# Reordering the opening and the block loop of a fused linear-attention and mixture-of-experts kernel, with the first expert matrix fetched in two halves

## The chip, the cores and the metric

The kernel runs on one core of a Trainium2 chip. The metric is device time of one execution in microseconds (us). A quoted median is over the executions of one kernel on one chip; a ratio is the mean time of one kernel's fast runs over the mean of the other's fast runs of the same rounds, so it is not quite the ratio of the two medians. Ratios carry a 95% interval in square brackets. Some executions of a kernel fall in a slower state, at a lower clock; the record marks an execution as slow when it is over 1.5% above the fastest of its kernel, and only fast ones are compared. Engines are PE (matmuls), PEld (PE's weight loads), DVE, ACT, POOL and SP; SP and POOL also issue DMA transfers here.

## The reference, cut

```python
# attention: r, k, v are (B=4, H=8, S=768, D=48), w and u are (H, D)
for t in range(S):
    cur = einsum('bhd,bhe->bhde', u * k[:, :, t], v[:, :, t])
    y[:, :, t] = einsum('bhd,bhde->bhe', r[:, :, t], state + cur)
    state = w[..., None] * state + einsum('bhd,bhe->bhde', k[:, :, t], v[:, :, t])
x = y.transpose(0, 2, 1, 3).reshape(4, 768, 384)
# one expert out of 8 for each batch entry (a whole sentence)
logits = x.mean(axis=1) @ w_gate
e = argmax(logits, axis=1)
gate_w = softmax(logits)[e]
out[b] = gate_w[b] * (relu(x[b] @ w1[e[b]]) @ w2[e[b]])     # w1 (8,384,1024), w2 (8,1024,384)
```

Which expert's weights batch b needs is known only when all of x[b] has been computed. So each batch has a moment, the *gate*, from which its weights can first be fetched.

## The kernel before

The sequence is cut into 12 blocks of 256 rows, three for each batch. A block goes through scaling of k and r (POOL), transposes (PE) copied out by ACT, scores (PE) masked by DVE, outputs and state (PE), and transposing back. After the third block of a batch come the gate, three small DVE instructions and the weight transfers, which POOL issues. One batch of expert work is 28 *jobs*: 16 of the first layer (`mm1`, which need w1) and 12 of the second (`mm2`). They stand in a list, and the block loop takes some at each `slot()`.

```python
    def gate(b):
        ...                                        # 3 matmuls into lgp
        lg = gpool.tile([128, E], FP32, tag="lg", name=f"lg{b}")
        nc.vector.tensor_copy(lg, lgp[:, 0:E])
        ...
        nc.vector.max(out=top8, in_=lg)
        nc.vector.max_index(out=idx8, in_max=top8, in_values=lg)

    def weights(b):
        ev = nc.gpsimd.value_load(idx8[0:1, 0:1], min_val=0, max_val=E - 1)
        w1 = wpool.tile([128, NCT, F], BF16, tag="w1", name=f"w1_{b}")
        nc.gpsimd.dma_start(out=..., in_=moe_w1[ds(ev, 1)]...)
        w2 = ...
        nc.gpsimd.dma_start(out=..., in_=moe_w2[ds(ev, 1)]...)
        ...
        jobs.append(lambda ft=ft, sb=sb: mm1(b, w1, ht, ft, sb))     # x16
        jobs.append(lambda ...: mm2(b, w2, ht, si, half, cell, obs)) # x12

    RATE = 8.5 / 7
    acc = [0.0, False]

    def slot():
        if acc[1]:
            acc[0] += RATE
            c = int(acc[0])
            acc[0] -= c
            moe(c)                 # the next c jobs of the list
        else:
            fill(2, 256)           # matmuls on zeros

    for g in range(NB, N):         # blocks 3 to 11; blocks 0 to 2 are written out above
        ...                        # scaling for a later block; conditions for the last blocks are left out
        transposes(g + 1, 0)
        slot()
        scores_v(g, 1, True)
        slot()
        transposes(g + 1, 1)
        ...
        scores_v(g, 0, gi == 0); add_bonus(g); evac_y(g, 0)
        slot()
        inter(g, 1); evac_y(g, 1); scores(g + 1, 0)
        slot()
        backs(g)
        slot()
        acc[1] = True              # jobs begin in block 3, after its fifth slot
        if last:
            gate(b)
            weights(b)
        scores(g + 1, 1)
        slot()
        bonus(g + 1)
        slot()
    moe(len(jobs))
```

## Time and profile before

| what | value |
|---|---|
| median of 4 executions, beside the changed kernel's | 154.63 us (154.41 to 156.17) |
| span of the profiled execution | 152.6 us |
| PE busy | 139.5 us, 91% |
| ACT, DVE, POOL busy | 83.6, 74.4, 68.5 us |
| first expert job on PE | 45.04 us |

The head of the page's second part, span and two rows of 40 equal slices, shows where PE is not full. The first row is PE's busy share in tenths, the second the granted PE clock in tenths.

```profile
span 152.6 us, 4539 instructions
...
PE   6999877956989999999999999999999999999991
...
PEclk9999999995599999999999999999999999999999
```

PE is full from the thirteenth slice on, and the clock drops to half for about two slices in the opening.

### The profile page before, as it was taken

The numbers are of one execution on the slowest core, as the hardware profiler recorded it, in microseconds if no ns is written. First come the engines' busy times: TensorE is split into PE (matmuls) and PEld (weight loads), VectorE is DVE, ScalarE is ACT, GpSimd is POOL, SyncE is SP. The second block draws the span as 40 slices with busy tenths as digits, with TensorE's granted clock in tenths as the row PEclk, the third lists the DMA queues.
The fourth block names the chain that finished last, engine by engine and source line by source line (L and its number), as shares of the span: only waits on it lengthen the run. The fifth ranks groups of instructions, "written<-read, shape, count | busy, mean of one in ns | idle before, by whom it ended". The sixth has DMA issues, their size and how long they took to land.

```text
span 152.6 us, 4539 instructions
## 1 busy us (share of the span) xinstructions
PE 139.5 (91%) x1951; PEld 97.9 (64%) x1951; DVE 74.4 (49%) x164; ACT 83.6 (55%) x144; POOL 68.5 (45%) x62
## 2 busy tenths in 40 slices
PE   6999877956989999999999999999999999999991
PEld 2266645644767878766677877666777765676560
DVE  7837796125465654754548456465562321121110
ACT  0976567351356766546476784563664543556231
POOL 4169659207976839289292862963021020000000
PEclk9999999995599999999999999999999999999999
DMA  2999998303999999999991000998020079960034
GB/s 59 301 322 321 279 268 226 99 0 92 227 215 297 249 312 269 293 214 210 215 376 48 4 0 4 153 195 267 22 93 4 0 111 208 161 247 0 0 126 185
DMA packets 41464, 25.47 MB, mean 167 GB/s; under 512 B 38755, under 2 KB 39012, under 8 KB 41444
## 3 DMA queue, kind: packets, MB, share of 16 engines
q1 hardware_dynamic: 39460, 18.89, 42.9%
q0 software_dynamic: 1152, 6.29, 22.3%
q8 instruction: 15, 0.25, 0.6%
q10 hardware_dynamic: 832, 0.00, 0.3%
q14 instruction: 5, 0.04, 0.1%
HBM read 26.76 MB, written 4.72 MB: 206 GB/s over the span
## 4 chain that ended last, share of the span: by engine, by line
PE 78%; DVE 10%; ACT 8%; issue 2%; DVEq 0%
PE op L503 21%; PE hp L483 21%; PE twp L236 7%; PE at L260 5%; DVE gt L268 5%; PE fill L113 5%; PE y L353 5%; ACT kr L246 4%; PE s L361 2%; PE xp L402 2%; ACT ht L490 2%; PE y L313 2%; PE y L323 2%; DVE ht L492 1%; DVE st L376 1%
## 5 line engine op out<-in xcount | busy, mean ns | idle before, releaser
L483 PE MATMUL hp<-xt,w 128*128 128x384 bf16 x192 | 41.4, 334 | 1.3 <-DVE lg L436 0.3
L503 PE MATMUL op<-w,ht 128*128 128x384 bf16 x192 | 34.9, 326 | 0.1
L246 ACT COPY kr<-twp 128x1024 bf16<-128x1024 bf16 x24 | 24.1, 1011 | 18.4 <-PE twp L236 18.4
L268 DVE TENSOR_TENSOR gt<-at,mask 128x1024 bf16<-128x1024 f32 x24 | 29.3, 1221 | 8.8 <-PE at L260 8.6
L490 ACT ACTIVATE ht<-hp 128x384 bf16<-128x384 f32 x48 | 23.4, 491 | 17.8 <-PE hp L483 17.1
L483 PEld LDWEIGHTS <-w 128*128 128x128 bf16 x192 | 25.0, 148 | 8.1 <-issue 4.4
L305 POOL TENSOR_TENSOR vt<-vb,tcol 128x768 bf16<-128x768 bf16 x11 | 16.3, 1477 | 25.4 <-DVE tcol L297 25.4
L503 PEld LDWEIGHTS <-ht 128*128 128x128 bf16 x192 | 17.3, 97 | 11.1 <-issue 0.8
L247 DVE TENSOR_TENSOR prod<-twp,kr 128x512 bf16<-128x512 bf16 x24 | 10.2, 424 | 27.8 <-ACT kr L246 27.8
L199 POOL TENSOR_TENSOR kp<-k,dk 128x768 bf16<-128x768 f32 x11 | 20.0, 1816 | 1.4 <-DMA k<-in_k_dram 1.4
L199 POOL TENSOR_TENSOR rp<-r,dr 128x768 bf16<-128x768 f32 x11 | 20.0, 1820 | 0.0
L510 ACT ACTIVATE ob<-op,gw 128x384 f32<-128x384 f32 x16 | 9.3, 581 | 13.2 <-PE op L503 12.9
L113 PE MATMUL fill<-zero 128*128 128x512 bf16 (+1 forms) x45 | 14.5, 430 | 1.9 <-DVE zero L85 1.3
L353 PEld LDWEIGHTS <-gt 64*128 64x128 bf16 x384 | 11.5, 94 | 5.0 <-issue 3.9
L492 DVE TENSOR_SCALAR ht<-hp 128x384 bf16<-128x384 f32 x16 | 8.9, 554 | 11.7 <-PE hp L483 11.5
L353 PE MATMUL y<-vb,gt 64*128 64x48 bf16 x384 | 14.1, 182 | 0.4 <-ACT xn L389 0.4
L260 PE MATMUL at<-kr 48*64 48x128 bf16 x384 | 10.5, 229 | 3.6 <-ACT kr L246 1.7
L389 ACT CAST xn<-y 128x384 bf16<-128x384 f32 x24 | 11.1, 480 | 4.1 <-PE y L323 3.5
L462 POOL DMA_DIRECT2D w<-in_moe_w_dram x4 | 2.5, 623 | 22.5 <-DVE gw L452 7.8
L260 PEld LDWEIGHTS <-kr 48*64 48x64 bf16 x384 | 7.0, 110 | 8.2 <-issue 6.2
L410 ACT COPY xt<-xp 128x768 bf16<-128x768 bf16 x12 | 9.6, 798 | 4.3 <-PE xp L402 4.3
L361 PE MATMUL s<-vb,kp 64*128 64x96 bf16 x160 | 10.5, 208 | 0.4 <-DVE st L376 0.4
(73 smaller groups left out, 155.6 us busy)
## 6 DMA issues: line engine op xcount, KB each, us to landing
w<-in_moe_w_dram POOLq DMA_DIRECT2D x8, 768.0 KB, 10.2
k<-in_k_dram SPq DMA_DIRECT2D x12, 384.0 KB, 5.1
r<-in_r_dram SPq DMA_DIRECT2D x12, 384.0 KB, 5.8
v<-in_v_dram SPq DMA_DIRECT2D x12, 384.0 KB, 5.7
out_dram<-ob SPq DMA_DIRECT2D x11, 384.0 KB, 5.6
out_dram<-ob SPq DMA_DIRECT2D x2, 192.0 KB, 1.9
wuT<-in_w_dram ACTq DMA_DIRECT2D x2, 0.8 KB, 3.6
wuT<-in_u_dram ACTq DMA_DIRECT2D x2, 0.8 KB, 4.1
```

What stands on the lines that cost most here:

```text
L113: nc.tensor.matmul(out=fills[-1][:, 0:cols], lhsT=zero[:, 0:128], rhs=zero[:, 0:cols], start=True, stop=True)
L199: eng.tensor_mul(dst[:, cs, :, 0:D].rearrange("q c h d -> q h c d"), src[:, :, cs, :], dec[:, :, cs, :])
L246: nc.scalar.copy(kts[g][:, :, :, c, :], tw)
L260: nc.tensor.matmul(out=at[64 * j : 64 * j + 64, a, pp, cs, :], lhsT=kt[q, p, j, cs, :], rhs=rt[q, p, j].rearrange("q c i -> q (c i)"), sta ...
L268: nc.vector.tensor_mul(gts[g][:, rnd].rearrange("q a p c t -> q (a p) c t"), at.rearrange("q a p c t -> q (a p) c t"), mask.rearrange("q n ...
L305: nc.gpsimd.tensor_mul(vt, vbs[g].rearrange("q c h d -> q (c h) d"), tcol.to_broadcast([128, 2 * H, D]))
L353: nc.tensor.matmul(out=yj[:, D * h : D * h + D], lhsT=gt[q, p // 2, a, p % 2, c, :], rhs=vb[q, c, h, :], start=(first and i == 0), stop=(c ...
L361: nc.tensor.matmul(out=sp[:, 96 * p : 96 * p + 96], lhsT=kp[g % NR][qo, c, 2 * p : 2 * p + 2, :].rearrange("s a b -> s (a b)"), rhs=vb[qo, ...
L389: nc.scalar.copy(xns[g][:, j, :], ys[g][j][:, 0:DM])
L483: nc.tensor.matmul(out=hp[:, 0:SB], lhsT=w1[:, ct, ft::NFT], rhs=xts[b][:, ct, SB * sb : SB * sb + SB], start=(ct == 0), stop=(ct == NCT - 1),
L490: nc.scalar.activation(out=o, in_=hp[:, 0:SB], func=ACT.Relu)
L503: nc.tensor.matmul(out=op[:, 0:DM], lhsT=ht[:, ft, 128 * si : 128 * si + 128], rhs=w2[:, ft, :], start=(ft == 0), stop=(ft == NFT - 1),)
```

## The change

The intent is to make the first expert job early (k and r of the first blocks are loaded ahead of v; w1 comes in two halves so that the first jobs need only one) and to have each block's transposes and first scores done well before they are needed. The DVE copy of the logits goes. The diff, cut to its core:

```diff
-    load(0)
-    load(1)
+    load(0, "kr")
+    load(1, "kr")
+    load(0, "v")
+    load(2, "kr")
+    load(1, "v")
+    load(2, "v")
 ...
-        lg = gpool.tile([128, E], FP32, tag="lg", name=f"lg{b}")
-        nc.vector.tensor_copy(lg, lgp[:, 0:E])
+        lg = lgp[:, 0:E]
 ...
-        w1 = wpool.tile([128, NCT, F], BF16, tag="w1", name=f"w1_{b}")
-        nc.gpsimd.dma_start(out=w1..., in_=moe_w1[ds(ev, 1)]...)
+        w1 = []
+        for fh in range(2):
+            t = wpool.tile([128, NCT, HF], BF16, tag=f"w1_{fh}", name=f"w1_{b}_{fh}")
+            nc.gpsimd.dma_start(
+                out=t,
+                in_=moe_w1[ds(ev, 1)].rearrange("o (p ct) f -> p (o ct) f", ct=NCT)[
+                    :, :, HF * fh : HF * fh + HF])
+            w1.append(t)
 ...
-                out=hp[:, 0:SB], lhsT=w1[:, ct, ft::NFT],
+                out=hp[:, 0:SB], lhsT=w1[ft // 4][:, ct, ft % 4 :: 4],
 ... the written-out opening of blocks 0 to 2, reordered; scores_v split so that
 ... outputs and state matmuls can stand apart; then the loop:
     for g in range(NB, N):
 ... scaling for a later block; conditions for the last blocks are left out
+        scores_v(g, 1)
+        scores(g + 1, 0)
+        slot()
+        transposes(g + 2, 0); prod(g + 2, 0)
+        acc[1] = True
+        slot()
+        slot()
+        inter(g, 0); scores_v(g, 0); add_bonus(g)
+        scores(g + 1, 1)
+        inter(g, 1); evac_y(g, 0); evac_y(g, 1)
+        slot()
+        slot()
+        backs(g)
+        ...
+        slot()
+        if last:
+            gate(b)
+            weights(b)
+            gate_weight(b)
+        transposes(g + 2, 1); prod(g + 2, 1)
+        slot()
+        slot()
```

The new body has eight slots where the old one had seven, `RATE` is not touched, and jobs begin in block 3 before its second slot instead of after its fifth.

## The prediction

> **What bounds the kernel now.** I read the page's sliced rows first, then stretches of the span, then the chain of work that ended last. One line each for the opening (two of them), the loop and the tail, from the view of stretches (columns: stretch, length, then busy us of PE, PEld, DVE, ACT, POOL, then the granted clock):
>
> ```profile
> core 0: us, PE busy (x) PEld busy (x) DVE busy (x) ACT busy (x) POOL busy (x), PEclk, DMA share, GB/s
> ...
> 7.90:30.30 22.40, 19.40 (x394) 13.31 (x393) 13.37 (x21) 13.93 (x23) 15.40 (x9) 1.00 0.94 254
> 30.30:45.00 14.70, 10.84 (x194) 8.06 (x191) 7.32 (x18) 6.51 (x9) 9.62 (x8) 0.77 0.60 127
> 45.00:123.50 78.50, 77.40 (x1217) 58.19 (x1210) 42.57 (x90) 47.98 (x84) 41.07 (x32) 1.00 0.64 160
> 123.50:152.60 29.10, 25.24 (x145) 16.10 (x142) 4.70 (x8) 11.01 (x21) 0.00 (x0) 1.00 0.52 134
> ```
>
> From 45.0 to 123.5 us PE is busy 77.4 of 78.5 us, so there only fewer or better packed PE instructions help. Before 45 us PE waits on hand-overs (PE, ACT, DVE and back), runs fill matmuls, and at 30 to 45 us even loses the clock (0.77). So a gain must make the first expert job run earlier than 45.0 us. The rest of the change permutes a saturated PE stream.
>
> What matters most is how the expert weights are fetched. The route is known only when the gate matmuls (tile lgp) of a batch are done. The chain shows them thrice in the loop:
>
> ```profile
> 62.70 0.65 PE lgp L431 x6
> ...
> 91.84 0.83 PE lgp L431 x6
> 92.67 0.35 PE at L260 x16
> 93.02 0.64 PE hp L483 x3
> ...
> 94.39 0.45 PE twp L236 x8
> ...
> 119.46 0.63 PE lgp L431 x6
> ```
>
> and this is what follows the second on DVE and POOL, and, in a fence of its own, the landing of its first weight transfer (least, median, most):
>
> ```profile
> 92.71 0.17 DVE L436 COPY lg<-lgp 128x8 f32<-128x8 f32 x1 [0.93 <-PE lgp L431]
> ...
> 93.19 0.16 DVE L440 FIND_INDEX8 idx<-top,lg 128x8 uint32<-128x8 f32 x1
> ...
> 94.58 0.59 POOL L462 DMA_DIRECT2D w<-in_moe_w_dram  x1 [4.26 <-DVE tcol L297]
> ```
>
> ```profile
> DMA to landing us min/median/max: 6.4/6.4/6.4
> ```
>
> The matmuls end at 92.67, the transfer is issued at 94.58 (1.91 us later) and w1 lands 6.4 us after that: 8.3 us from gate to weights. The issues of the first and third gates in the loop come 1.94 and 1.97 us after theirs; w1 landed 9.0 and 6.4 us after issue, the 9.0 beside input loads. PE does not stop for it today because old jobs are queued. Counting slots in the program (7 per block, 8.5/7 jobs each, 28 jobs per batch: 16 first-layer, 12 second-layer), 12, 14 and 17 jobs remain at the three gates.
>
> **What the Trainium skill says.** "TensorE: Matmul & The Clock Gate", Part 2, step 1: matmuls stay in program order, only weight loads are pulled ahead. The trace agrees: its PE timeline is the program's order. So a matmul that waits for w1 stops everything behind it. "DMA: Bandwidth & Descriptors", "Anatomy of one DMA — SWDGE (gpsimd) path": about 2.0 us plus bytes/436e3. For w1's 1.57 MB read that is 5.6 us; the trace has 6.4, so I use the trace. Same page, "Issuing engines are not separate DMA queues": all issuers share 16 engines; the 9.0 us beside loads agrees. The TensorE page, "HAM oscillation — how this bites in real kernels": avoid PE gaps over about 3.4 us or the clock halves. The trace shows it harsher: with only partial gaps (0.55 and 1.38 us) around 33 to 35 us the clock was 0.50 from about 35 to 41 us.
>
> **The change part by part.**
>
> Opening. Order k0 r0 k1 r1 instead of k0 r0 v0 k1 brings k1 one 384 KB transfer ahead. POOL waited 1.44 us for it and began the scaling of block 1 at 9.16 us; now about 7.8. Two fewer fills of 0.43 us let the first transposes start at 6.9 rather than 7.67, and DVE takes the second of the two ACT copies (1.93 us for both in a row), so the first scores run near 9.9 instead of 10.93. From there I followed the new program order by hand with durations from the timeline (copy of transposes 1.01, masking of scores 1.22, product 0.42, state 0.55, output cast 0.48, POOL scaling 1.82). Block 0 stays 1 us ahead; block 1 loses most of it because products and state sit on DVE's queue before the masking (second masking of block 1 again at about 19.3); the finer order of block 2's outputs then gains: last output cast near 27.9, the gate's matmuls near 28.6 to 29.3 instead of 31.5 to 32.3, and without the wait of the 0.16 us logits copy behind a product (33.09) the weights issue at about 31.3 instead of 35.32: 4 us earlier.
>
> But the loop needs more before its first job: transposes of block 3 and 4 and half of 5. On POOL, behind three weight issues (about 2 us to 33.5), come rp4 1.82, vb4 0.82, vt3 1.47, kp5 and rp5 3.64: 41.3 us. So the first job starts at about 41.6, not 45.04 (half of w1 has landed by 37). At that point the old kernel had more of block 3 and 4 behind it: outputs 0.52, bonus add 0.29, second state part 0.25, transposing back 0.55, scores 0.35, less one transposition pass 0.45 = 1.5 us. Net gain 45.0 - 41.6 - 1.5 = 1.9 us.
>
> Loop. Work per block is the same, and PE is full, so transposes ahead gain nothing by themselves. But the new body has 8 slots per block where the old had 7, with the same 8.5/7 jobs each, and starts jobs at slot 2 of block 3. So it uses 9.7 jobs per block. Counting again: at the three gates 3, 2 and 1 old jobs remain (26 after the loop instead of 42). The moved jobs cost PE the same later or sooner. The new first-layer jobs, however, meet weights that are not there.
>
> Time from gate to half of w1: 1.91 less the removed logits copy (0.17) = 1.75; landing: 6.4 is about 1.3 until packets flow (in the second fetch DMA traffic begins near 95.9) and 5.1 of transfer; half is 1.3 + 2.55, plus 0.3 that I allow for runs of 2 KB instead of 12: 4.2. Together 6.0 us (an estimate).
>
> What PE has meanwhile: transposes 0.45, an old second-layer job 0.65 (four matmuls in the chain: 0.65 to 0.76), outputs 0.52, scores 0.35.
> - Gate 1: 0.45 + 2 x 0.65 + 0.52 + 0.35 + 0.65 = 3.3, stop of 2.7 us.
> - Gate 2: 0.45 + 2 x 0.65 = 1.75, stop of 4.2.
> - Gate 3: 0.65, stop of 5.4.
>
> Sum 12.3 us, wholly on the path. Second halves land some 2.6 us after the first, under the 8 jobs (5 us) that use the first; w2 about 13.5 us after the gate, under the 16 jobs. Neither waits.
>
> Clock. Stops over 4 us will probably drop the clock for some 3.4 us, each costing 1.7; I take 2.0 in all. Tail: 4 fewer first-layer jobs at 0.62 instead of 0.55: -0.3.
>
> **Sum.** 154.7 - 1.9 + 12.3 + 2.0 - 0.3 = 166.8; I say 166.5.
>
> **The rivals.**
> (a) The opening gain carries through and the kernel ends 2 to 4 us earlier (about 151 to 153). For it: half w1 is on purpose made early, the gate's chain gets shorter, and the opening is where PE has slack. Against: it would need the gate-to-weights time to fall from 8.3 to 2 us or less, and halving one transfer leaves 1.75 us of issue and over 1.3 of start.
> (b) Nothing moves (about 155): the weights arrive sooner because no input loads are left by then and the stops shrink to 1 us each, offset by the opening. Against: 6.4 us was measured without loads already.
> (c) Worse: each stop also halves the clock for longer, as the 6 us at 35 to 41 in the old trace, and the split transfers of 384 short runs take POOL longer to issue: 3 x 3 for the clock and 3 x 1 for the issue, about 173.
>
> **Range and chances.** The stops are sure in sign if my slot count is right: even with a landing 3 us after issue (gate to half of w1 4.75) they sum to 1.5 + 3.0 + 4.1 = 8.6. Opening gain may be 0 to 4. So 160 to 172. Faster by over 2%: 0.05 (count or order misread). Within 2%: 0.05. Slower: 0.90.
>
> **What would show it.** In the changed profile: gate matmuls of batch 0 near 29 us, first expert matmul near 41 to 42; PE's sliced row broken in three places, just after the later lgp groups, with idle of about 3, 4 and 5 us before first-layer matmuls, ended by the DMA of w; clock below 1 after them; tail from the last gate to the end 27 to 29 us instead of 32.5. I am wrong if PE stays at 9 tenths in the loop or idles before anything other than those matmuls; the opening part is wrong if the first expert matmul starts later than 44 us.

## More of the kernel before

The gates of the three batches inside the loop stand on PE's timeline (start, length, instruction, then the idle time before it):

```profile
62.54 0.81 PE L431 MATMUL lgp<-wg,pooled 128*128 128x8 f32 x6
...
91.84 0.83 PE L431 MATMUL lgp<-wg,pooled 128*128 128x8 f32 x6 [0.22 <-DVE pooled L420]
...
119.30 0.78 PE L431 MATMUL lgp<-wg,pooled 128*128 128x8 f32 x6
```

PE does not stop after any of them: jobs of the batch before are still in the list there (the prediction counts them) and need no new weights.

## The result, and the profile after

The changed kernel took 179.22 us (178.37 to 183.08, four executions) beside 154.63 us for the kernel before. The ratio of the fast runs is 1.1547 [1.1429, 1.1665]. It is correct and much slower, and it lies outside the predicted range of 160 to 172.

The execution profiled with this result was the slow one of the four. Its rows of slices:

```profile
PE   7986679979699999946998999239899992199992
...
PEclk9998555556999999995799999965999999559999
```

So the same kernel was run once more unedited (experiment a_ctrl), and there the profile fell on a fast execution. All further lines of "after" are from that one. The head of its page:

```profile
span 179.6 us, 4505 instructions
...
PE   7975688978999999918998999149899991299992
...
PEclk9999955557999999995899999956999998559999
```

Against the old rows: PE has three holes, at slices 18, 26 and 34 to 35. Behind each hole the clock is low for about two slices. And the half clock in the opening lasts longer than before, 22.1 to 42.5 us. PE's timeline names the holes: the gate matmuls of batches 1 and 3, and the first first-layer job after each of the three gates (the end of a line is the idle time of PE before it, and what ended that).

```profile
72.88 0.73 PE L481 MATMUL lgp<-wg,pooled 128*128 128x8 f32 x6
...
81.56 1.15 PE L538 MATMUL hp<-xt,w 128*128 128x384 bf16 x3 [4.57 <-DMA w<-in_moe_w_dram]
...
119.11 1.14 PE L538 MATMUL hp<-xt,w 128*128 128x384 bf16 x3 [6.36 <-DMA w<-in_moe_w_dram]
...
147.43 0.73 PE L481 MATMUL lgp<-wg,pooled 128*128 128x8 f32 x6
...
156.22 1.15 PE L538 MATMUL hp<-xt,w 128*128 128x384 bf16 x3 [7.40 <-DMA w<-in_moe_w_dram]
```

All three stops are waits for the DMA of w, and together they are 4.57 + 6.36 + 7.40 = 18.3 us. The chain of waits across the third gate (start, length, what) tells the rest of that time apart:

```profile
146.94 0.65 PE op L558 x4
147.59 0.58 PE lgp L481 x6
...
148.19 0.19 DVE top L487
...
148.40 0.24 DVE idx L489 x2
...
148.71 0.26 POOLq L510
...
149.37 0.48 issue
...
149.88 6.29 DMA w<-in_moe_w_dram
...
156.22 1.79 PE hp L538 x5
```

From the end of the gate matmuls, 148.17, to the issue of the first half, 149.88, pass 1.71 us; from there to the landing 6.29. At the other two gates the first half landed 6.1 and 6.3 us after its issue. Before, the whole of w1 took 6.4 at the gate that the prediction showed, so the half came hardly sooner than the whole had; a_whole below compares the two in one kernel. The landing times of the two halves of the second gate (least, median, most, us from issue):

```profile
DMA to landing us min/median/max: 6.3/7.0/7.6
```

The view of stretches shows what the first stop leaves behind:

```profile
core 0: us, PE busy (x) PEld busy (x) DVE busy (x) ACT busy (x) POOL busy (x), PEclk, DMA share, GB/s
77.00:81.56 4.56, 0.01 (x1) 0.01 (x1) 0.59 (x1) 0.58 (x1) 4.54 (x4) 0.84 1.03 134
81.56:86.90 5.34, 5.34 (x61) 3.29 (x61) 1.54 (x3) 2.06 (x4) 0.45 (x1) 0.50 1.11 242
86.90:92.00 5.10, 5.10 (x86) 3.80 (x75) 2.41 (x5) 4.33 (x8) 2.63 (x2) 1.00 0.07 13
```

The weights are there from 81.56 on and PE is busy without a break, but at clock 0.50, for 5.34 us; it gets through 61 instructions where the next 5.10 us hold 86. The same happens after the other stops, for 5.39 and 5.78 us.

Last, the opening: the gate matmuls of batch 0 and the first expert job.

```profile
32.41 1.39 PE L481 MATMUL lgp<-wg,pooled 128*128 128x8 f32 x6
...
47.34 1.14 PE L538 MATMUL hp<-xt,w 128*128 128x384 bf16 x6
```

Before, they stood at 31.5 and 45.04. Both came later, not earlier.

### The profile page after: what moved, and what is told of

Its sections match the earlier page's. It is cut to its first block, busy times and chain, and to the rows that moved or that the text cites. A ratio compares the mean times of both kernels' runs of the same rounds, so it can differ in the third digit from the quotient of the medians.

```text
span 181.4 us, 4509 instructions
## 1 busy us (share of the span) xinstructions
PE 148.7 (82%) x1938; PEld 97.8 (54%) x1938; DVE 76.1 (42%) x162; ACT 83.3 (46%) x142; POOL 73.6 (41%) x66
## 3 DMA queue, kind: packets, MB, share of 16 engines
q0 software_dynamic: 4288, 6.29, 20.7%
## 4 chain that ended last, share of the span: by engine, by line
PE 66%; DMA 10%; ACT 9%; DVE 6%; POOL 4%; issue 3%; POOLq 1%; DVEq 0%; ACTq 0%
PE hp L538 19%; PE op L558 15%; DMA w<-in_moe_w_dram 10%; PE twp L241 6%; PE fill L118 5%; PE y L361 4%; PE at L271 3%; ACT ht L545 3%; ACT kr L254 3%; DVE gt L279 3%; PE y L339 3%; PE s L387 2%; PE xp L455 2%; PE y L349 2%; POOL vt L316 2%
## 5 line engine op out<-in xcount | busy, mean ns | idle before, releaser
L538 PE MATMUL hp<-xt,w 128*128 128x384 bf16 x192 | 43.4, 363 | 19.8 <-DMA w<-in_moe_w_dram 17.9
L538 PEld LDWEIGHTS <-w 128*128 128x128 bf16 x192 | 21.1, 120 | 33.4 <-DMA w<-in_moe_w_dram 19.1
L254 ACT COPY kr<-twp 128x1024 bf16<-128x1024 bf16 x23 | 23.1, 1011 | 22.7 <-PE twp L241 22.6
L279 DVE TENSOR_TENSOR gt<-at,mask 128x1024 bf16<-128x1024 f32 x24 | 29.3, 1220 | 6.5 <-PE at L271 6.5
L361 PEld LDWEIGHTS <-gt 64*128 64x128 bf16 x384 | 12.2, 98 | 7.1 <-issue 6.3
L361 PE MATMUL y<-vb,gt 64*128 64x48 bf16 x384 | 15.0, 188 | 0.0
L515 POOL DMA_DIRECT2D w<-in_moe_w_dram x8 | 6.4, 806 | 21.1 <-DVE gw L501 21.1
L118 PE MATMUL fill<-zero 128*128 128x512 bf16 (+1 forms) x32 | 13.5, 539 | 1.3 <-DVE zero L87 1.3
L241 PE MATMUL twp<-ident,kp 128*128 128x128 bf16 x96 | 11.3, 252 | 2.5 <-DVE prod L258 2.0
L271 PE MATMUL at<-kr 48*64 48x128 bf16 x384 | 11.4, 245 | 1.5 <-ACT kr L254 0.9
L387 PE MATMUL s<-vb,kp 64*128 64x96 bf16 x160 | 11.7, 222 | 0.8 <-DVE tcol L308 0.8
```

The source lines that it names most:

```text
L118: nc.tensor.matmul(out=fills[-1][:, 0:cols], lhsT=zero[:, 0:128], rhs=zero[:, 0:cols], start=True, stop=True)
L241: nc.tensor.transpose(out=twp[:, o + p, :], in_=src[:, c, 2 * p : 2 * p + 2, :].rearrange("s a b -> s (a b)"), identity=ident,)
L254: nc.scalar.copy(kts[g][:, :, :, c, :], tw)
L271: nc.tensor.matmul(out=at[64 * j : 64 * j + 64, a, pp, cs, :], lhsT=kt[q, p, j, cs, :], rhs=rt[q, p, j].rearrange("q c i -> q (c i)"), sta ...
L279: nc.vector.tensor_mul(gts[g][:, rnd].rearrange("q a p c t -> q (a p) c t"), at.rearrange("q a p c t -> q (a p) c t"), mask.rearrange("q n ...
L361: nc.tensor.matmul(out=yj[:, D * h : D * h + D], lhsT=gt[q, p // 2, a, p % 2, c, :], rhs=vb[q, c, h, :], start=begin(g, j), stop=(c == 1), ...
```

## The experiments

The theory: the job pacing (eight slots at the old rate, and the earlier start) empties the list at the gates, PE stops for the weights, and the stop lowers the clock. The rivals: the new order of the loop or the opening is itself slower; or the splitting of w1 is what makes the weights late. All twelve kernels gave correct results. "Changed" below is the kernel after the change; diffs are against the kernel named.

### a_ctrl: the changed kernel again

No edit.

> The changed kernel again, unedited, to have its trace in the fast state. All theories: 178 to 180 us. Theory 1 (the stops for w1): the three idles of PE that a w transfer ends sum to 17 to 19 us also here, so they are not an accident of the slow profile. Theory 2 (the opening's lost clock): the clock is at half from about 18 to 44 us as in the slow profile; if the opening keeps the clock here, theory 2 can explain only the slow execution's extra 4.6 us.

Measured: 181.45 us beside 154.7, ratio 1.1736 [1.161, 1.1862], span 179.6 us, mean clock 0.875. Its lines are shown above. The stops repeat: 18.3 us here, 17.9 in the slow profile. The ratio is 1.9 points higher, with overlapping intervals. So the result is no accident of one execution. The next runs are read against this ratio.

### a_pace: the changed kernel at eight jobs per block

```diff
-    RATE = 8.5 / 7
+    RATE = 1.0
```

This leaves 7, 11 and 15 jobs in the list at the three gates, by the same count of slots, instead of 3, 2 and 1.

> The changed kernel with one number changed: 1.0 jobs per slot (8 per block) instead of 8.5/7 (9.7 per block), so that 7, 11 and 15 old jobs remain at the three gates instead of 3, 2 and 1. Theory 1: no PE idle before first-layer matmuls, the half clock after the stops gone too; 179 - 18 - 4 = 157 us (155 to 160). Theory 2: at most half of the loss is the stops, so above 165. Theory 3 (the new order inside the block costs PE itself): above 162 with PE idle in the loop at other places.

Measured: 156.35 us (155.34 to 156.91), ratio 1.008 [0.9977, 1.0183]. PE no longer waits for w at any gate: its list of waits names no transfer of w. The page's rows:

```profile
PE   6987777986978999999999999999999999999990
...
PEclk9999955555589999999999999999999999999999
```

One number takes away nearly the whole loss. The loop is now as full as before, so the new order of the loop is not slower by itself, and w1 still comes in halves, so the splitting is not what costs the time. The half clock in the opening (19.6 to 43.5 us) stays, and with it the kernel is no better than before.

### b_pace: the kernel before, paced as the change paces

```diff
-    RATE = 8.5 / 7
+    RATE = 1.4
 ...
         evac_y(g, 0)
+        acc[1] = True
         slot()
 ...
         slot()
-        acc[1] = True
```

It has 9.8 jobs per block, and 5, 3 and 2 jobs left at the gates. Nothing else of the change is in it.

> The kernel before with the pace alone of the change: 1.4 jobs per slot from slot 3 of block 3, so that 5, 3 and 2 jobs remain at the gates instead of 12, 14 and 17; opening, order and whole w1 as before. Theory 1: three stops before first-layer matmuls of about 4, 5 and 7 us, with 2 to 4 us of half clock: 170 to 176 us. Theories 2 and 3: near 155 to 160.

Measured: 180.12 us (178.75 to 183.42), ratio 1.1591 [1.1439, 1.1743]. The rows and the group of waits (total us, number, longest):

```profile
PE   7988798478999999439999999079999990298992
...
PEclk9999969966999999975999999957999997559999
```

```profile
PE hp L483 <- DMA w<-in_moe_w_dram: 19.6, 4, 7.9
```

The old kernel gets the same three holes, 5.42, 5.48 and 7.95 us, the same low clock behind each, and nearly the same loss (a fourth, small wait of 0.75 us is at batch 0). With a_pace this settles the main cause from both sides: pacing alone makes the loss, and undoing the pacing alone takes it away.

### a_whole: the changed kernel with w1 in one transfer

```diff
-        w1 = []
-        for fh in range(2):
-            t = wpool.tile([128, NCT, HF], BF16, ...)
-            nc.gpsimd.dma_start(out=t, in_=...[:, :, HF * fh : HF * fh + HF])
-            w1.append(t)
+        w1 = wpool.tile([128, NCT, F], BF16, tag="w1", name=f"w1_{b}")
+        nc.gpsimd.dma_start(
+            out=w1.rearrange("p ct f -> p (ct f)"),
+            in_=moe_w1[ds(ev, 1)].rearrange("o (p ct) f -> p (o ct f)", ct=NCT))
 ... w2 in the old layout, and mm1 with the old column step
```

> The changed kernel with w1 fetched whole and both weights in the old layout. If the halves bring the first half in sooner by the time of half a transfer (2.5 us, as the prediction had it) this is 3 x 2.5 = 7 us slower than the changed kernel, 186. If halves don't land sooner, because the transfers of both halves run beside each other and short runs are slower (first half 6.4 us after issue in the changed kernel's trace, whole w1 6.4 in the old one's), it is the same within 2 us.

Measured: 181.96 us, ratio 1.1771 [1.165, 1.1892], stops 5.21, 7.34 and 8.07:

```profile
PE hp L534 <- DMA w<-in_moe_w_dram: 20.6, 3, 8.1
```

The landing at the second gate:

```profile
DMA to landing us min/median/max: 7.3/7.3/7.3
```

The whole landed 6.8, 7.3 and 6.9 us after its issue at the three gates, the half 6.1 to 6.3. The stops are 20.6 - 18.3 = 2.3 us longer, 0.6 to 1.0 us for each gate, where the prediction gave the halves 2.2 us each (6.4 - 4.2). The time differs by 0.3%, inside both intervals. So the halves bring under 1 us for each gate and nothing that the times can tell, nor do they cost anything.

### a_alone: the first half with nothing queued right behind it

```diff
             nc.gpsimd.dma_start(out=t, in_=...)
+            if fh == 0:
+                for _ in range(4):
+                    nc.gpsimd.tensor_mul(scr, dk, dr)
```

Four throwaway multiplications on POOL (they slow this kernel; it was executed once, so its state is unknown) keep the second half and w2 back, so that the first half has the transfer engines nearly to itself.

> The changed kernel with four throwaway POOL multiplies (about 7 us) between the issue of the first half of w1 and that of the second half and w2, so that the first half travels alone. If the other transfers in the queue are what makes the first half land as late as a whole w1 (5.6 to 6.4 us after its issue), it lands about 4.2 us after. If start-up and short runs are, it still takes about 6. The time itself gets longer in both cases (second half and w2 some 7 us later), about 190 us.

Measured: 186.38 us. The first half landed 4.9, 6.3 and 4.9 us after its issue at the three gates of the loop. The first of them:

```profile
DMA to landing us min/median/max: 4.9/4.9/4.9
```

At the second gate, with 6.3, an output store was issued 0.7 us after it and moved in the midst of it; the changed kernel, with the same store there, has 6.3 too, so at this gate holding the rest back brought nothing. At the other two, where by the packet records hardly anything moved beside the half, it was 1.2 to 1.4 us quicker than the 6.1 to 6.3 of the changed kernel: there, more than half of what the prediction missed is that the second half and w2, issued right behind, share the engines with the first. The packet records of the first profile of the changed kernel agree: between the first and the last of the first half's sixteen completions pass 1.5, 0.8 and 2.1 us at the three gates, and by the last one 77 to 252 of the second half's 384 packets have begun. Some 0.7 us to the predicted 4.2 remain. A half is written as 384 packets of 1 KB at about 98 ns; over 16 engines that is 24 x 98 ns = 2.4 us. The whole w1 is 128 packets of 6 KB at 474 ns, 8 x 474 ns = 3.8 us, half of which is 1.9. The small packets can thus account for 0.5 us of the half's transfer (the prediction allowed 0.3). POOL's issuing instruction, too, takes 0.80 us for the first half and 0.59 for the whole w1 of a_whole, which can account for 0.2 more. The rest, some 0.3 us, stays open.

### a_stopfill: the changed kernel, with matmuls on zeros in the stops

```diff
     def mm1(b, w1, ht, ft, sb):
+        if b and ft == 0 and sb == 0:
+            fill_bank()
+            fill((0, 20, 29, 34)[b], 512)
```

The weights come as late as ever, but PE has something to do until they do. This separates the stop itself from the clock that falls in it.

> The changed kernel with 20, 29 and 34 fill matmuls put in just before the first first-layer matmul of batches 1, 2 and 3, so that PE spends the stops for w1 on fills (4.3, 6.3 and 7.3 us at the full clock) and the clock does not fall. Theory: of the 25 us between the changed kernel and its slow-paced form, 18 are the stops themselves and some 7 the half clock that follows each: 181.4 - 7 = 174 to 175 us. Rival (the 7 us are something else, such as the first half of w2 or ACT): 180 to 182.

Measured: 175.98 us (fast executions 174.49 to 176.09) beside 154.64, ratio 1.139 [1.1303, 1.1478], mean clock 0.937, and a clock of 1.0 from 41.9 to 171 us. The two stretches at the first gate, to be held against those of the changed kernel above:

```profile
core 0: us, PE busy (x) PEld busy (x) DVE busy (x) ACT busy (x) POOL busy (x), PEclk, DMA share, GB/s
76.50:81.40 4.90, 4.67 (x22) 1.99 (x22) 1.02 (x1) 0.58 (x1) 4.88 (x5) 1.00 0.96 123
81.40:87.00 5.60, 5.60 (x96) 4.26 (x97) 3.42 (x6) 3.87 (x8) 0.76 (x2) 1.00 1.11 241
```

In the stretch after the stop PE does 96 instructions in 5.60 us, where it did 61 in 5.34. The low clock after the stops is worth 1.1736 - 1.139 = 0.0346 of 154.7 us: 5.4 us, give or take 2. (Of the eleven executions of the kernel before beside this one, one took 306.71 us; it is left out. b_hold, a_best and a_hold5 are measured beside the same eleven.)

### a_hold: a_pace with more matmuls on zeros in the opening

a_pace left one visible fault, the half clock of the opening. The edit adds 32 matmuls on zeros to it where PE had gaps (the expectation says 26), and makes one that was 256 columns wide 512:

```diff
+    fill(2, 512)            # before scores_v(0, 1)
     scores_v(0, 1)
-    fill(1, 512)
+    fill(4, 512)
 ...
+    fill(3, 512)            # before bonus(1)
+    fill(6, 512)            # before turn_back(0)
+    fill(2, 512)            # before bonus(2, False)
+    fill(3, 512)            # after vt_mul(2)
+    fill(3, 512)            # before state_mms(2, 0)
+    fill(2, 512)            # before pool_mms(1)
-    fill(1, 512)            # after inter(2, 1)
+    fill(3, 512)
-    fill(1, 256)            # before pool_mms(2)
+    fill(2, 512)
-    fill(2, 512)            # after prod(3, 0)
+    fill(7, 512)
```

> The changed kernel at 1.0 jobs per slot with 26 more fill matmuls in the new opening, placed where PE idled, to keep the clock up from 19 to 43 us. Theory 1b (the new opening's gain is eaten by the half clock alone): the clock holds, the gate matmuls of batch 0 come near 29 us instead of 33, the first job near 45 instead of 48, and the time is 152 to 154 instead of 156.4. Rival (the opening is bound by hand-overs, not by PE's clock): gate matmuls still near 33 and 156 us or, with the fills in the way, more.

Measured: 152.8 us (152.4 to 153.62) beside 154.65, ratio 0.9891 [0.9802, 0.9981]; mean clock 0.997.

```profile
PE   6999999997769999999999999999999999999990
...
PEclk9999999999999999999999999999999999999998
```

The clock lost in the opening was therefore worth 1.008 - 0.9891 = 0.0189, 2.9 us (3.4 with the repeat a_hold5), give or take 2. The opening itself, at full clock now, can be read for the first time:

```profile
31.58 0.84 PE L481 MATMUL lgp<-wg,pooled 128*128 128x8 f32 x6
...
44.60 0.40 PE L241 MATMUL twp<-ident,rp 128*128 128x128 bf16 x4 [1.05 <-POOL rp L204]
44.83 1.14 PE L538 MATMUL hp<-xt,w 128*128 128x384 bf16 x6
...
67.02 0.73 PE L481 MATMUL lgp<-wg,pooled 128*128 128x8 f32 x6
...
93.58 0.73 PE L481 MATMUL lgp<-wg,pooled 128*128 128x8 f32 x6
...
118.84 0.73 PE L481 MATMUL lgp<-wg,pooled 128*128 128x8 f32 x6
```

The gate of batch 0 stands at 31.58 (before: 31.5; expected: 29) and the first job at 44.83 (before: 45.04). The new opening, even undisturbed by the clock, starts the experts no earlier. The added fills may hold it up a little, so this is a reading and no proof; a_oldhold below tests it. The gates of the loop are 26.6 and 25.3 us apart with 24 jobs between them. Before, they were 29.3 and 27.5 apart with 26 and 25 jobs. Taking the difference of 2 and 1 jobs at about 0.65 us, the new loop needs 29.3 - 1.3 - 26.6 = 1.4 and 27.5 - 0.65 - 25.3 = 1.5 us less for three blocks, about 0.5 us for one (an estimate from these two profiles). The second distance repeats: it is 25.3 in all six traces of the new loop at 8 jobs per block, and 27.5 again in b_hold, which has the old loop.

### a_hold5: the same kernel, five rounds

No edit to a_hold.

> The slow-paced, fill-held changed kernel again with more rounds, on the same chip as the old kernel with held clock: 152.8, that is 1 to 1.5% below the kernel before.

Measured: 152.66 us (152.4 to 153.58), ratio 0.9862 [0.9806, 0.9918]. The gain is clear of noise: 0.8 to 1.9%.

### b_hold: the kernel before, with more matmuls on zeros in its opening

```diff
+    fill(3, 512)
     transposes(3, 0)
     gate(0)
 ...
     transposes(3, 1)
-    fill(2, 256)
+    fill(8, 512)
     scores(3, 0)
-    fill(2, 256)
+    fill(5, 512)
     scores(3, 1)
```

> The kernel before with 16 more fill matmuls from 30 to 37 us, where its clock falls to half till 41 us. If the half clock costs the old kernel something too, it gets up to 1 us faster (153.6); if its opening waits on w1 (landing at 43.5 us) and on hand-overs anyway, 154.6. Either tells what the fair comparison for the fill-held changed kernel (152.8) is.

The edit adds 12 and widens four (the expectation says 16). Measured: 153.59 us (153.25 to 155.58), ratio 0.9913 [0.9858, 0.9967]. The profiled execution was a slow one and still shows a half clock from 27.2 to 34.0, so it isn't compared with the others line by line. The old kernel, too, had 0.9% to win in its opening. Next to it, a_hold's 0.986 to 0.989 is 0.2 to 0.5% ahead, inside the intervals: the loop's gain is seen in the distances of the gates, and isn't separated by the times.

### a_oldopen: the opening of before ahead of the loop of the change

```diff
-    load(0, "kr") ... load(2, "v")          # loads as before
+    load(0)
+    load(1)
-    RATE = 8.5 / 7
+    RATE = 1.0
 ... the written-out opening of before, then what the new loop needs besides:
 ... transposes of blocks 4 and half of 5
```

> The loop of the change (transposes two blocks ahead, scores beside the outputs, w1 in halves) at 1.0 jobs per slot behind the opening and load order of the kernel before. In the slow-paced changed kernel a batch between two gates took about 2.7 us less than in the kernel before for 2 jobs less (1.2 us), so the loop's order seems to save some 0.5 us a block. Theory 4 (the loop's order gains 4 us over nine blocks and the new opening loses them): 150 to 153 us, below the kernel before. Rival (the loop gains nothing, as the prediction had it): 155 to 158.

Measured: 156.63 us (156.34 to 156.86), ratio 1.0125 [1.0043, 1.0207]. Inconclusive: the clock was half from 28.9 to 49.3, and PE stood before a transpose that POOL had not scaled for:

```profile
41.26 0.61 PE L238 MATMUL twp<-ident,rp 128*128 128x128 bf16 x4 [2.53 <-POOL rp L201]
```

The order in which I put POOL's work made that wait, so the run compares a poor joint and not the two openings. The fair form is a_oldhold.

### a_best: a_hold with POOL's order mended

In a_hold PE waits 1.05 us for POOL's scaling of r just before the first job, while POOL had stood idle for 6.75 us waiting for the gate. Scaling moved ahead of the gate uses that idle time:

```diff
     prep_k(4)
+    prep_r(4)
+    prep_v(4)
+    prep_k(5)
+    prep_r(5)
 ...
-    prep_r(4)
-    prep_v(4)
 ...
-    prep_k(5)
-    prep_r(5)
```

> The slow-paced, fill-held changed kernel (152.8 us) with POOL's scaling of blocks 4 and 5 moved ahead of the weight issue, where POOL sat idle for 6.75 us: in its trace the last transposes before the first job waited 1.05 us for POOL. Expected 151 to 152, if POOL is what bounds the stretch between gate and first job; unchanged if it is ACT's and DVE's hand-overs or w1's landing.

Measured: 152.05 us (151.33 to 152.83, six executions), ratio 0.9827 [0.9772, 0.9882], span 149.7 us. The first job:

```profile
42.79 1.14 PE L538 MATMUL hp<-xt,w 128*128 128x384 bf16 x6
```

It runs 2.0 us earlier than in a_hold, yet the ratio moves only 0.9862 - 0.9827 = 0.35%, 0.5 us, with overlapping intervals. Part of the two microseconds is lost again at the first gate of the loop, where PE now waits 0.75 us for w, a stop that a_hold did not have; the rest was not traced. This version beats both kernels: the kernel before by 1.2 to 2.3%.

### a_oldhold: the opening of before, held and mended alike, ahead of the loop of the change

a_oldopen with fills in the gaps and with the same POOL work moved ahead of the gate.

> The loop of the change at 1.0 jobs per slot behind the old opening, now with fills that hold the clock and POOL's scaling of blocks 4 and 5 ahead of the weight issue, as in the best variant. The variant with the old opening and no such fills (156.6 us) had lost the clock from 29 to 49 us and waited 2.5 us for POOL, so it could not tell what the loop's order is worth. If the loop's order alone makes the best variant faster than the old kernel and the new opening is worth nothing, this gives 152 us, the same as the best variant (152.05; 0.983 of the kernel before). If the new opening carries the gain, it gives 154 or more.

Measured: 153.16 us (152.06 to 157.21; the four fast ones of six 152.06 to 153.52) beside 154.81, ratio 0.9841 [0.978, 0.9903]. The profiled execution was slow (half clock 22.8 to 26.2) with the first job at 43.86. With like care, the old opening gives 0.984 and the new one 0.983, on two chips and with intervals of 0.6 points to either side. The reordered opening and loads are worth nothing that these runs can tell. The care was not quite equal: the profile of a_oldhold has a wait of 1.97 us for w at the first gate of the loop, against 0.75 in a_best.

## Why the prediction was wrong

The sign, the place and the cause were right; the size was not. The step that failed first of all is the time from the issue of the first half of w1 to its landing, put at 4.2 us and measured at 6.1 to 6.3; the cost of the clock and the gain of the opening were mis-sized as well. The prediction had +12.1 us as its sum of parts. The ratios of a_ctrl, a_stopfill and a_pace, times 154.7 us, split the measured loss; each difference carries an uncertainty of about 2 us, from the intervals. (The first measurement of the same kernel, 1.1547, makes the whole loss 23.9 us; the two intervals overlap. The parts are taken from runs with a_ctrl's ratio because its trace is the one shown.)

| part | predicted us | measured us | from |
|---|---|---|---|
| the three stops | +12.3 | +20.3 | a_stopfill less a_pace: 1.139 - 1.008 |
| half clock after the stops | +2.0 | +5.4 | a_ctrl less a_stopfill: 1.1736 - 1.139 |
| opening, loop and tail | -2.2 | +1.2 | a_pace: 1.008 |
| sum | +12.1 | +26.9 | a_ctrl: 1.1736 |

**Job count (right).** Stops come at exactly the three gates inside the loop, and only before first-layer jobs. a_pace and b_pace show that the pacing is both enough and needed.

**What PE has meanwhile (right).** After the first gate the timeline has transposes, eight and four second-layer matmuls (three jobs), outputs and scores; after the third one job. That is the predicted list.

**From gate to issue (right).** 1.75 predicted; 1.71 at the third gate.

**From issue to landing of half of w1 (the failed step).** It was put at 1.3 + 2.55 + 0.3 = 4.2 us; it took 6.1 to 6.3. That explains each stop by itself: 4.57, 6.36 and 7.40 are 1.9, 2.2 and 2.0 us over the predicted 2.7, 4.2 and 5.4. I halved a transfer's time as though the half moved alone, although I had cited that all transfers share the same engines; the second half and w2 were issued right behind it. a_alone shows 1.2 to 1.4 us of the error as this sharing at two gates of three; at the other, beside an output store, holding the rest back brought nothing. The small packets account for perhaps 0.2 us beyond the 0.3 allowed, the longer issue for perhaps 0.2, and the rest is open. The stop term measured by times, 20.3, is 2 us above the idle time of 18.3 that the trace shows; the intervals don't decide whether that is anything.

**Clock (under-sized).** I took about 3.4 us of half clock, hence 1.7 lost, per stop, and booked 2.0 for all. In the trace PE worked 5.34, 5.39 and 5.78 us at half clock, together 16.5 us, of which up to half is lost; a_stopfill priced it at 5.4 us. Rival (c) gave the clock 3 x 3 us, about as far over the measured as the prediction was under. It also expected a longer issue: the two halves do take POOL 1.6 us to issue where the whole w1 of a_whole takes 0.6, but only 0.2 us of that lie in the first half's own instruction, and PE never waits for the second half or w2. Its sum is wrong, too: with the prediction's other terms its 9 and 3 us make 154.7 - 1.9 - 0.3 + 12.3 + 9 + 3 = 176.8, not 173. It was nearest, for a partly wrong reason.

**Opening (wrong in sign).** I expected the gate's matmuls at 28.6 to 29.3 and the first job at 41.6. They came at 32.4 and 47.3 with the clock halved from 22.1 on, and at 31.6 and 44.8 with it held (a_hold). I followed hand-overs by hand at full clock and never asked whether the thinner PE stream would keep that clock: its loss is 2.9 to 3.4 us, give or take 2. What hand-over ate the other gain of 2 to 3 us was not taken apart; a_oldhold only shows that the new opening has no lead left.

**Loop.** "Gains nothing by itself" was slightly too dark: about 0.5 us per block by the distances of the gates. The times do not show it apart from the held clock of b_hold, and no run has the old loop at 8 jobs per block. Why the order is quicker was not taken apart.

**Tail.** From the last gate to the end I expected 27 to 29 us with a stop of 5.4. It is 179.6 - 147.4 = 32.2 with a stop of 7.40 and 5.78 us of half clock; less the 2.0 of longer stop and less some 2 us of clock, about 28. The work in it was right.

## What to carry to other kernels

When data can be fetched only once a decision is known, count in the program how much independent work is queued at that moment, and re-derive every pacing constant when the number of places that use it changes: here one untouched constant over one more slot and an earlier start cost most of the 26.9 us, and setting the constant again took all but 1.2 us of it away. A transfer cut in halves need not bring its first half in half the time while the rest is queued right behind it: here 6.1 to 6.3 us against 6.8 to 7.3 for the whole. And price a stop of PE as the idle time plus the half clock that follows it, and a reordering of a thin stretch with the clock that it may lose; matmuls on zeros are a cheap test of both.

## What the Trainium skill lacked or had wrong

- "DMA: Bandwidth & Descriptors", section "Anatomy of one DMA — SWDGE (gpsimd) path": 2.0 us plus bytes/436e3 gives, as an estimate, 3.8 us for half of w1 (0.79 MB read) and 5.6 us for all of it. At the gates of the loop the runs show 4.9 us for the half with hardly anything moving beside it (twice; 6.3 beside an output store), 6.1 to 6.3 us with two more transfers issued behind it, and 6.4 to 9.0 us for the whole (nine fetches in before, a_whole and b_pace). The page does say, in "Rules for kernel authors", that two transfers to disjoint partition halves share the same engines; it has no figure for when the first of several queued transfers lands.
- "TensorE: Matmul & The Clock Gate", section "What's actually happening", has full clock back after a busy window of about 3.4 us, and the window runs free of the kernel. Here it came back 5.3, 5.4 and 5.8 us after PE had restarted, so the 3.4 us are too few to price a restart with. The page is not contradicted: around the three stops the trace grants half clock for 6.8, 6.8 and 10.2 us, which is two, two and three times 3.4. The two values of the clock, half and full, agree with the page as well.
- The same page, "HAM oscillation — how this bites in real kernels", speaks of PE gaps longer than about 3.4 us; its next section, "A second HAM failure mode: psum-queue depth-cycling", says that frequent short idles can do it too, without a size. Here the clock of the opening was half for about 20 us (22.1 to 42.5) without any single idle of PE over about 1.4 us. With 32 more matmuls on zeros the mean clock of the whole run was 0.997, and the time fell from 1.008 to 0.986 to 0.989 of the kernel before.
